# Row sums of a head pair added on TensorE in one episode, and the order written anew around it

## The chip, the cores and the metric

One core of one Trainium2 chip runs the whole kernel in one launch. The metric is the device time of an execution in microseconds (us); a lower number is better. TensorE is called PE here, VectorE DVE, ScalarE ACT, GpSimd POOL and SyncE SP, as in the profile.

## The reference

Two stages follow each other. The first is attention over 8 batches and 8 heads, 1152 keys of 64 features, with queries averaged in pairs (576 per head). The second is a mixture of experts that sends each of the 4608 tokens to one of 8 experts.

```python
q_pool = q.reshape(B, H, S // 2, 2, D).mean(axis=3)
scores = scale * np.matmul(q_pool, k.transpose(0, 1, 3, 2))
scores = scores - np.max(scores, axis=-1, keepdims=True)
attn = np.exp(scores)
attn = attn / (np.sum(attn, axis=-1, keepdims=True) + 1e-09)
x = np.matmul(attn, v)            # then (B, S, H*D) as 4608 tokens of 512
logits = x @ w_gate; expert = argmax(logits); gate = softmax(logits)[expert]
out[token] = gate * (relu(x[token] @ w1[expert]) @ w2[expert])
```

## The kernel before

**Tiles of attention.** A batch has four pairs of heads, and a pair's 576 queries are taken in two halves of 288. For each half there are nine chunks of 128 keys. `scores` (L584 to L642) multiplies a chunk in one *score step*: four matmuls of 64 rows by 64 columns that stand in the four quarters of PE's array (L601). DVE takes the chunk out of PSUM into the tile `s` and keeps its minimum (L606). Then the minimum is spread over the partitions by PE (L624), a bias comes of it on DVE (L630), and ACT raises the half to exponentials in three instructions of three chunks each (L634). `values` (L703 to L721) multiplies the chunks with v, again four matmuls of 64 by 64 for a chunk, a *value step* (L714). Score chunks pass through two PSUM tiles `st`, so a third score step has to wait until DVE has taken the first.

**Row sums.** `chunk_sum` (L664 to L701) adds up the exponentials of a half. POOL folds nine chunks into three in two additions of 1728 numbers a partition (L681, L682, shown as line L680 in the profile, where the helper stands). In the first half of a pair a third addition of 576 numbers brings them down to two. PE then adds over the partitions with columns of ones, in matmuls of 128 rows by 32 columns: four of 288 queries in the first half (L692), four of 288 and four of 144 in the second (L692, L698). The matmuls between one change of shape and the next are called an *episode* here: 64x64 for scores and values, 128x32 for sums and router logits, 64x128 for the transposes of q and k (L546, L552). For the last three pairs of the last batch (`LAST = 3`) POOL is left out, and PE adds all nine chunks itself (`whole`, L670 to L678, shown as L675).

**A batch's sums.** `row_sums` (L723 to L745) copies the sums from PSUM (L729), turns and adds the two query halves of the array with three matmuls against the constant `sums_of` (L735), adds 1e-9 (L741) and takes the reciprocal (L742) into `rec`. `routing` (L760 to L909) then makes logits (L789), turns them (L796), picks experts, ranks the tokens, and has POOL write the tokens into the experts' lists by six indirect DMAs (L893). The token numbers lie in `tok`, which DVE raises by 576 for each batch (L855).

**Into the experts.** While the last batch of attention runs, `first_slots` (L911 to L951) picks the two fullest experts so far; SP loads a list for each, and POOL gathers their tokens (L994). The last batch's list writes wait for those gathers. After attention PE runs the experts' products (L1211, L1242, L1272).

**What sets the order.** Nothing is scheduled by the compiler. `Flow.add` takes steps with an engine, a planned duration, a key and the steps that they wait for, and `Flow.emit` (L120 to L236) plays them through on a clock of its own. Each engine takes the ready step with the lowest key; on PE a step of the shape that stands is preferred to a step of another one, unless its key is higher by more than `KEEP`. The order that comes out is written into the program and does not change at run time. The keys come from the table at L30 to L50.

## Time and profile before

| | |
|---|---|
| median of 3 runs | 1170.93 us (1168.75 to 1171.44) |
| the profiled execution's own time | 1169.15 us |
| its span, first to last instruction | 1167.6 us |
| granted clock of TensorE, mean | 0.996 |
| busy: PE, DVE, ACT, POOL | 98%, 67%, 55%, 69% of the span |

The profile has one execution. Attention takes the stretch up to the last value step, which ends near 717 us; the experts take the rest. In a row of the timeline stand the start, the time until the end of the last instruction, the engine, the line, and what was done how often. PE's matmuls overlap, so the time that a piece takes is the start of the next row less its own start. An fp32 matmul leaves two records, so a step of four matmuls is a row with x8.

### The profile page before, as it was taken

What the parts mean: (1) busy time and instruction counts of PE and PEld (TensorE: products, weight loads), DVE (VectorE), ACT (ScalarE), POOL (GpSimd) and SP (SyncE); (2) the same over time, 40 slices, a digit from 0 to 9 for tenths busy, and PEclk for the clock granted to TensorE, in tenths of its full rate; (3) what the DMA queues carried; (4) which work ended last, traced back from release to release, by engine and by line L of the source; (5) the groups of instructions that cost most, each with busy time, mean ns of one, the idle gap of its engine ahead of it and who ended that gap; (6) DMA issues with size and microseconds to landing.
All of it is one profiled execution on the core that took longest, in us unless ns stands there. A gap on an engine that the chain in (4) does not pass through costs nothing.

```text
span 1167.6 us, 34514 instructions
## 1 busy us (share of the span) xinstructions
PE 1148.6 (98%) x14431; PEld 822.3 (70%) x14431; DVE 778.7 (67%) x2141; ACT 636.4 (55%) x794; POOL 808.7 (69%) x440
## 2 busy tenths in 40 slices
PE   8999999999999999999999999999999999999996
PEld 4565555566566556556556566889998989999985
DVE  6777867868868768768768777975554554636440
ACT  4667667567567667667667457433333342535440
POOL 3989899899899899899899334456656566641010
PEclk9999999999999999999999999999999999999998
DMA  7644334344344344344254334754444344625320
GB/s 183 154 116 115 100 89 122 107 97 124 98 105 123 90 109 121 89 117 127 75 122 130 83 97 124 201 179 122 130 123 128 119 133 119 196 72 181 120 71 20
DMA packets 78052, 138.15 MB, mean 118 GB/s; under 512 B 11321, under 2 KB 35777, under 8 KB 77888
## 3 DMA queue, kind: packets, MB, share of 16 engines
q1 hardware_dynamic: 67904, 115.96, 36.2%
q0 software_dynamic: 9712, 19.64, 5.8%
q8 instruction: 115, 1.88, 0.8%
q14 instruction: 49, 0.40, 0.1%
q10 hardware_dynamic: 272, 0.26, 0.1%
HBM read 115.04 MB, written 21.02 MB: 117 GB/s over the span
## 4 chain that ended last, share of the span: by engine, by line
PE 92%; DVE 4%; issue 2%; ACT 0%; POOL 0%; POOLq 0%; ACTq 0%; DVEq 0%
PE st L601 24%; PE m L714 24%; PE ph L1211 16%; PE py L1272 12%; PE py L1242 5%; PE sums L692 3%; PE st L546 2%; DVE s L606 2%; PE sums L675 1%; PE st L552 1%; DVE w2l L1117 1%; PE st L624 1%; PE sums L789 1%; PE sums L698 1%; PE m L1261 0%
## 5 line engine op out<-in xcount | busy, mean ns | idle before, releaser
L606 DVE TENSOR_SCALAR_CACHE_REDUCE s<-st 128x576 f32<-128x576 f32 x576 | 420.7, 753 | 138.5 <-PE st L601 130.9
L634 ACT ACTIVATE s<-s,bias 128x1728 f32<-128x1728 f32 x192 | 320.1, 1730 | 139.6 <-DVE bias L630 110.1
L601 PE MATMUL st<-qT,kT 64*64 64x288 f32 x4608 | 361.7, 408 | 2.5 <-DVE s L606 1.9
L714 PE MATMUL m<-s,vn 64*64 64x288 f32 x4608 | 356.6, 404 | 0.0
L601 PEld LDWEIGHTS st<-qT,kT 64*64 64x64 f32 x4608 | 163.8, 132 | 134.2 <-DVE s L606 54.5
L714 PEld LDWEIGHTS m<-s,vn 64*64 64x64 f32 x4608 | 172.2, 133 | 86.0 <-issue 1.7
L680 POOL TENSOR_TENSOR fold<-s 128x1728 f32<-128x1728 f32 x58 | 224.3, 3867 | 8.5 <-ACT s L634 8.2
L680 POOL TENSOR_TENSOR fold<-fold,s 128x1728 f32<-128x1728 f32 x58 | 225.0, 3880 | 1.8
L994 POOL DMA_INDIRECT xr<-x_runs,ix x99 | 108.1, 1092 | 87.4 <-DVE s L606 20.9
L1211 PE MATMUL ph<-xh,w1h 128*128 128x384 f32 (+6 forms) x480 | 150.3, 313 | 1.6 <-ACT xh L1162 0.8
L1211 PE MATMUL ph<-xl,w1h 128*128 128x384 f32 (+6 forms) x480 | 148.8, 310 | 0.3 <-DVE xl L1117 0.3
L1211 PE MATMUL ph<-xh,w1l 128*128 128x384 f32 (+6 forms) x480 | 148.4, 309 | 0.0
L1280 POOL DMA_INDIRECT out_dram<-y,rec x41 | 46.2, 1127 | 142.1 <-ACT hh L1218 46.6
L1220 DVE SCALAR_TENSOR_TENSOR hl<-ph,hh 128x384 fp32r<-128x384 f32 (+5 forms) x100 | 55.1, 551 | 98.7 <-ACT hh L1218 98.3
L1218 ACT ACTIVATE hh<-ph 128x384 fp32r<-128x384 f32 (+5 forms) x100 | 48.7, 487 | 122.8 <-PE ph L1211 122.7
L1211 PEld LDWEIGHTS ph<-xh,w1h 128*128 128x128 f32 x480 | 90.6, 189 | 4.3 <-DVE hl L1220 1.7
L1211 PEld LDWEIGHTS ph<-xl,w1h 128*128 128x128 f32 x480 | 90.5, 189 | 1.1 <-DVE xl L1117 0.5
L1211 PEld LDWEIGHTS ph<-xh,w1l 128*128 128x128 f32 x480 | 90.3, 188 | 0.0
L1272 PE MATMUL py<-w2h,hh 128*128 128x512 f32 x224 | 88.7, 396 | 0.0
L1272 PE MATMUL py<-w2h,hl 128*128 128x512 f32 x224 | 88.3, 394 | 0.0
L1272 PE MATMUL py<-w2l,hh 128*128 128x512 f32 x224 | 88.0, 393 | 0.0
L893 POOL DMA_INDIRECT lists<-re,di x48 | 44.7, 931 | 60.1 <-PE m L714 33.1
(190 smaller groups left out, 1442.1 us busy)
## 6 DMA issues: line engine op xcount, KB each, us to landing
raw<-in_moe_w_dram SPq DMA_DIRECT2D x80, 512.0 KB, 4.4
qn<-in_q_dram SPq DMA_DIRECT2D x62, 384.0 KB, 5.6
vn<-in_v_dram SPq DMA_DIRECT2D x32, 576.0 KB, 4.0
kn<-in_k_dram SPq DMA_DIRECT2D x31, 576.0 KB, 5.2
x_runs<-row SPq DMA_DIRECT2D x96, 99.0 KB, 4.3
xr<-x_runs,ix POOLq DMA_INDIRECT x99, 2.7
x_runs<-empty SPq DMA_DIRECT2D x4, 297.0 KB, 7.9
xq<-x_runs,ix POOLq DMA_INDIRECT x49, 2.7
```

Of the source, the lines that this page charges most:

```text
L601: made = nc.tensor.matmul(pt.t[to, h, :HQ], x.kT.t[up, c * P + i * D:c * P + (i + 1) * D], x.qT.t[up, cols], start=True, stop=True, tile_p ...
L606: nc.vector.tensor_scalar(s.t[:, c], pt.t[:, :, :HQ], -SCALE, None, op0=ALU.mult, op1=ALU.min, accum_out=mx.t[:, c:c + 1],)
L634: nc.scalar.activation(s.t[:, c0:c0 + n], s.t[:, c0:c0 + n], AF.Exp, bias=bias.t, scale=-1.0)
L680: add = lambda to, a, b: nc.gpsimd.tensor_tensor(to, a, b, ALU.add)
L714: made = nc.tensor.matmul(pa[i].t[cs, :HQ], x.vn.t[up, h, c, :], s.t[up, c, h], start=c == 0, stop=c == NC - 1, tile_position=(up.start, c ...
L994: return nc.gpsimd.indirect_dma_start(out=x.xr[i // NQD].t[:, i % NQD, :], out_offset=None, in_=xg, in_offset=bass.IndirectOffsetOnAxis(ap ...
L1211: made = nc.tensor.matmul(view()[:, i, :], a[:, c, fp], b[:, c, :n], start=c == 0 and k == 0, stop=c == NDC - 1 and k == 2)
L1218: a = f.add("ACT", act(nb * n) - 44, lambda fs=fs, view=view: nc.scalar.activation(hidden(m)[0][:, fs, :n], view(), AF.Relu), at - 20, don ...
L1220: d = f.add("DVE", dve(nb * n), lambda fs=fs, view=view: nc.vector.scalar_tensor_tensor(hidden(m)[1][:, fs, :n], view(), 0.0, hidden(m)[0] ...
L1242: made = nc.tensor.matmul(py.t[:, :n], a[:, c % 2, ds], b[:, c, :n], start=c == 0 and k == 0, stop=c == NFC - 1 and k == 2)
L1272: made = nc.tensor.matmul(py.t[:n], a[:, c, hs], b[:, c % 2, :], start=c == 0 and k == 0, stop=c == NFC - 1 and k == 2)
L1280: ins = nc.gpsimd.indirect_dma_start(out=out, out_offset=bass.IndirectOffsetOnAxis(ap=x.re.t[:up, r:r + 1], axis=0), in_=y.t[:up], in_offs ...
```

## The change

The two halves of a pair are summed on PE in one piece. POOL folds the first half into `two`, by three additions of 1152 numbers and one of 576, and the second half into `three` as before. PE then runs four matmuls for `two` and eight for `three` behind each other. `LAST` is 2, so one more pair of the last batch is folded on POOL. A batch's sums are turned by three transposes instead of matmuls with `sums_of`; DVE adds the two query halves in one reduction from PSUM, and the small constant (now 0.5e-9 for each half) comes in as the bias of ACT's copy. Token numbers of all batches lie in a table `toks`, so `tok` is no longer raised. The last batch's list writes wait until the early lists are loaded, no longer until the gathers are done. Most keys of the table have new values, and the planned price of a change of shape is 130 in place of 110.

```diff
-FOLD_BUFS = 2
+TWO_BUFS, THREE_BUFS = 2, 1
-K_EXP = 13
-K_SUM = 33
+K_EXP = 37.8
+K_SUM = 25.6
...
-K_FIRST = 51
+K_FIRST = 78.3
...
-LAST = 3
+LAST = 2
...
-SWITCH = 110
+SWITCH = 130
...
-        u = tile_of(o, "fold", [P, 3, 2, HQ], bufs=FOLD_BUFS, pool=o.rt)
         add = lambda to, a, b: nc.gpsimd.tensor_tensor(to, a, b, ALU.add)
+        if half == 0:
+            u = tile_of(o, "two", [P, 2, 2, HQ], bufs=TWO_BUFS, pool=o.rt)
+            p = f.add("POOL", pool(4 * HQ), lambda: add(u.t, s.t[:, 0:2], s.t[:, 2:4]), key, every(ready[:4]), [s, u])
+            for c in (4, 6):
+                p = f.add("POOL", pool(4 * HQ), lambda c=c: add(u.t, u.t, s.t[:, c:c + 2]), key, done(p, *every(ready[c:c + 2])), [s, u])
+            p = f.add("POOL", pool(2 * HQ), lambda: add(u.t[:, 0], u.t[:, 0], s.t[:, 8]), key, done(p, ready[8]), [s, u])
+            sums.two = u, p
+            return None
+        u = tile_of(o, "three", [P, 3, 2, HQ], bufs=THREE_BUFS, pool=o.rt)
         p = f.add("POOL", pool(6 * HQ), lambda: add(u.t, s.t[:, 0:3], s.t[:, 3:6]), key, every(ready[:6]), [s, u])
         p = f.add("POOL", pool(6 * HQ), lambda: add(u.t, u.t, s.t[:, 6:9]), key, done(p, *every(ready[6:])), [s, u])
-        three = half
-        if not three:
-            p = f.add("POOL", pool(2 * HQ), lambda: add(u.t[:, 0], u.t[:, 0], u.t[:, 2]), key, done(p), [u])
+        u2, p2 = sums.two
 
         def total():
...
+            for i, h in grid:
+                put(i, h, 0, u2.t[:, i, h], start=hp == 0, stop=False)
+            for i, h in grid:
+                put(i, h, 1, u.t[:, i, h], start=False, stop=False)
+            for i, h in grid:
+                w = slice(i * HQ // 2, (i + 1) * HQ // 2)
+                put(i, h, 1, u.t[:, 2, h, w], w, start=False, stop=last)
 
-        return f.add("PE", 750 if three else 500, total, key + 15, done(p, *last), [u, sums], COLS)
+        return f.add("PE", 1235, total, key + 15, done(p, p2, *last), [u, u2, sums], COLS)
...
-        p = f.add("ACT", act(HQ) - 44, lambda: nc.scalar.copy(sm.t, sums.t[:, :HQ]), key, summed, [sums, sm])
+        p = f.add("ACT", act(HQ) - 44, lambda: nc.scalar.activation(sm.t, sums.t[:, :HQ], AF.Identity, bias=tiny), key, summed, [sums, sm])
...
-                nc.tensor.matmul(sums.t[:QP, HQ + j * NS:HQ + (j + 1) * NS], sm.t[:, j * QP:(j + 1) * QP],
-                                 sums_of.rearrange("p f a h -> p (f a h)"), start=True, stop=True)
+                nc.tensor.transpose(sums.t[:QP, j * P:(j + 1) * P], sm.t[:, j * QP:(j + 1) * QP], ident)
...
-            nc.vector.tensor_scalar(gs.t, src, 1e-9, None, op0=ALU.add)
-            nc.vector.reciprocal(rec.t.rearrange("p a j h -> p (a j h)"), gs.t.rearrange("p a j h -> p (a j h)"))
+            src = sums.t[:QP, :3 * P].rearrange("p (j u x z) -> p j x u z", j=3, u=2, x=2 * H)[:, :, :, :, 0]
+            nc.vector.tensor_reduce(gs.t, src, axis=AX.X, op=ALU.add)
+            nc.vector.reciprocal(rec.t.rearrange("p f j (a h) -> p j h a f", h=2),
+                                 gs.t.rearrange("p j (h a f) -> p j h a f", h=2, f=2))
...
-        i = f.add("ACT", 200, lambda: nc.scalar.copy(re.t.bitcast(I32)[:, :, 0], tok), at, done(*ready), [re])
+        i = f.add("ACT", 200, lambda: nc.scalar.copy(re.t.bitcast(I32)[:, :, 0], tok if b is None else toks[:, b]), at, done(*ready), [re])
...
-            outs.append(f.carry("POOL", 1230, lambda j=j: enlist(j), at + (K_PUT if b is None or b < B - 2 else 0) * j / NJ, done(p, i, *hold), [di, re], 40, 4400, paced=CALM))
+            outs.append(f.carry("POOL", 1230, lambda j=j: enlist(j), at + (K_PUT if b is None or b < B - 2 else 0) * j / NJ, done(p, i, *listed), [di, re], 40, ENLISTED if b == B - 2 else 4400, paced=CALM))
```

Three places show what became of the order. The first is PE in the second pair of a middle batch, before, where the first half's sums (`fold_5700`) stand between score steps (`st`); value steps are `m`, shown as two rows of x2.

```order
L601 MATMUL st_5899<-qT_5736,kT_5734 64x288 x4
L601 MATMUL st_5905<-qT_5736,kT_5734 64x288 x4
L692 MATMUL sums_5682<-fold_5700,ones_72 32x288 x4
L601 MATMUL st_5917<-qT_5736,kT_5734 64x288 x4
L714 MATMUL m_5855<-s_5568,vn_5013 64x288 x2
L714 MATMUL m_5858<-s_5568,vn_5013 64x288 x2
```

The same pair now: the first half's sums (`two_5689`) stand with the second half's, ahead of the transposes of a later pair's k.

```order
L606 MATMUL st_5962<-qT_5752,kT_5750 64x288 x4
L606 MATMUL st_5967<-qT_5752,kT_5750 64x288 x4
L701 MATMUL sums_5699<-two_5689,ones_72 32x288 x4
L701 MATMUL sums_5699<-three_5853,ones_72 32x288 x4
L701 MATMUL sums_5699<-three_5853,ones_72 32x144 x4
L551 MATMUL st_5991<-ident,kp_5771 128x64 x2
```

The lone piece is gone, and the joint piece has grown by one row.

The second place is PE a few steps behind a middle batch's router logits, as it was.

```order
L714 MATMUL m_5379<-s_5099,vn_4745 64x288 x2
L601 MATMUL st_5530<-qT_5360,kT_5358 64x288 x4
L601 MATMUL st_5543<-qT_5360,kT_5358 64x288 x4
L714 MATMUL m_5548<-s_5213,vn_4745 64x288 x2
L714 MATMUL m_5551<-s_5213,vn_4745 64x288 x2
```

And now:

```order
L725 MATMUL m_5372<-s_5132,vn_4787 64x288 x2
L606 MATMUL st_5540<-qT_5364,kT_5360 64x288 x4
L606 MATMUL st_5550<-qT_5364,kT_5360 64x288 x4
L606 MATMUL st_5565<-qT_5364,kT_5360 64x288 x4
L725 MATMUL m_5570<-s_5237,vn_4787 64x288 x2
L725 MATMUL m_5573<-s_5237,vn_4787 64x288 x2
```

Two score steps in a row have become three.

The third place is POOL in that second pair, before; `qp` is the pooling of a later pair's queries, `lists` a list write.

```order
L680 TENSOR_TENSOR fold_5700<-s_5406 128x1728
L893 DMA lists<-re_5423,di_5644 42240x2
L680 TENSOR_TENSOR fold_5700<-fold_5700,s_5406 128x1728
L680 TENSOR_TENSOR fold_5841<-s_5568 128x1728
L680 TENSOR_TENSOR fold_5700<-fold_5700 128x576
L680 TENSOR_TENSOR fold_5841<-fold_5841,s_5568 128x1728
L498 TENSOR_TENSOR qp_5949<-qn_5455 128x2x6x64
```

And now:

```order
L684 TENSOR_TENSOR two_5689<-s_5456 128x1152
L903 DMA lists<-re_5403,di_5665 42240x2
L684 TENSOR_TENSOR two_5689<-two_5689,s_5456 128x1152
L903 DMA lists<-re_5403,di_5665 42240x2
L684 TENSOR_TENSOR two_5689<-two_5689,s_5456 128x1152
L684 TENSOR_TENSOR three_5853<-s_5608 128x1728
L684 TENSOR_TENSOR two_5689<-two_5689,s_5456 128x576
L684 TENSOR_TENSOR three_5853<-three_5853,s_5608 128x1728
L503 TENSOR_TENSOR qp_5960<-qn_5393 128x2x6x64
```

POOL runs six additions for the pair where it ran five, and a list write has moved in between.

## Rows read from the trace of the kernel before

**Rows 1.** The page, busy time of each engine over the whole span.
```profile
PE 1148.6 (98%) x14431; PEld 822.3 (70%) x14431; DVE 778.7 (67%) x2141; ACT 636.4 (55%) x794; POOL 808.7 (69%) x440
```

**Rows 2.** The page, the chain that ended last, shares by engine.
```profile
PE 92%; DVE 4%; issue 2%; ACT 0%; POOL 0%; POOLq 0%; ACTq 0%; DVEq 0%
```

**Rows 3.** Waits of PE and its weight loads: total us, times, longest us.
```profile
PE st L601 <- DVE s L606: 1.9, 8, 0.4
...
PEld sums L692 <- POOL fold L680: 5.3, 12, 0.5
```

**Rows 4.** Timeline of PE, 336 to 349 us, one pair's two sum pieces.
```profile
339.52 1.20 PE L601 MATMUL st<-qT,kT 64*64 64x288 f32 x16
340.66 0.69 PE L692 MATMUL sums<-fold,ones 128*32 128x288 f32 x8
341.28 0.71 PE L601 MATMUL st<-qT,kT 64*64 64x288 f32 x8
341.82 0.67 PE L714 MATMUL m<-s,vn 64*64 64x288 f32 x8
342.30 0.67 PE L601 MATMUL st<-qT,kT 64*64 64x288 f32 x8
...
345.21 0.67 PE L601 MATMUL st<-qT,kT 64*64 64x288 f32 x8
345.81 0.69 PE L692 MATMUL sums<-fold,ones 128*32 128x288 f32 x8
346.32 0.43 PE L698 MATMUL sums<-fold,ones 128*32 128x144 f32 x8
346.68 0.27 PE L546 MATMUL st<-ident,kp 64*128 64x64 f32 x2
```

**Rows 5.** Timeline of PE, 300 to 326 us: both halves' sums in one piece.
```profile
303.56 1.18 PE L692 MATMUL sums<-fold,ones 128*32 128x288 f32 x16
304.56 0.43 PE L698 MATMUL sums<-fold,ones 128*32 128x144 f32 x8
```

**Rows 6.** Timeline of PE, 690 to 713 us, sums of all nine chunks by PE.
```profile
698.67 2.62 PE L675 MATMUL sums<-s,ones 128*32 128x288 f32 x36
701.22 1.20 PE L601 MATMUL st<-qT,kT 64*64 64x288 f32 x16
```

**Rows 7.** Groups of instructions: count, then busy us, mean ns; then idle before.
```profile
L735 PE MATMUL sums<-sums_of,sm 128*96 128x16 f32 x48 | 5.5, 240 | 0.5 <-ACT sm L729 0.5
L796 PE MATMUL sums<-ident,sm 128*96 128x128 f32 x24 | 4.2, 284 | 0.0
L606 DVE TENSOR_SCALAR_CACHE_REDUCE s<-st 128x576 f32<-128x576 f32 x576 | 420.7, 753 | 138.5 <-PE st L601 130.9 <-PE st L624 2.1
L606 DVE DVE_READ_ACCUMULATOR s<-st 128x1 f32 x576 | 47.6, 83 | 0.0
L634 ACT ACTIVATE s<-s,bias 128x1728 f32<-128x1728 f32 x192 | 320.1, 1730 | 139.6 <-DVE bias L630 110.1 <-POOL fold L680 24.7 <-DVE xr L1154 4.8
```

**Rows 8.** Timeline of PE, 660 to 668 us, a run of five score steps.
```profile
663.07 1.39 PE L601 MATMUL st<-qT,kT 64*64 64x288 f32 x16
664.67 1.40 PE L601 MATMUL st<-qT,kT 64*64 64x288 f32 x16 [0.21 <-DVE s L606]
```

**Rows 9.** Line L680 on POOL: instructions, duration ns min/median/max.
```profile
L680 POOL TENSOR_TENSOR fold<-s x58: 3846/3868/3892, 23.7 to 637.1; 128x1728 f32<-128x1728 f32 x58
L680 POOL TENSOR_TENSOR fold<-fold,s x58: 3845/3882/3912, 27.7 to 641.0; 128x1728 f32<-128x1728 f32 x58
L680 POOL TENSOR_TENSOR fold<-fold x29: 1394/1414/1437, 33.3 to 635.7; 128x576 f32<-128x576 f32 x29
```

**Rows 10.** Busy us of PE, PEld, DVE, ACT, POOL between two batches' logits; clock, DMA.
```profile
288.29:375.02 86.73, 86.70 (x1468) 51.80 (x1464) 66.05 (x199) 57.30 (x65) 79.69 (x31) 1.00 0.42 107
```

**Rows 11.** Timeline of all engines, 296 to 305 us: a spread and its exponentials.
```profile
296.86 0.29 PE L624 MATMUL st<-ident,top 64*64 64x64 f32 x8
...
297.81 4.99 ACT L634 ACTIVATE s<-s,bias 128x1728 f32<-128x1728 f32 x3 [2.53 <-DVE bias L630]
```

**Rows 12.** Timeline of POOL, 600 to 735 us, the first early gather.
```profile
679.00 1.05 POOL L994 DMA_INDIRECT xr<-x_runs,ix  x1 [20.92 <-DVE s L606]
```

More of the change, by code (lines that the diff above doesn't have):

```diff
@@ L56 @@
 LEAD = 55
-AHEAD = 152
+AHEAD = 144.8
 XR2 = 4
@@ L62 @@
 KEEP = 19
-LAST = 3
+LAST = 2
+LISTED = 1500
+ENLISTED = 800
 EXPS = 3
@@ L80, in __init__ @@
         self.kind, self.make, self.left, self.held, self.tile, self.slot = kind, make, 0, False, None, None
+        self.two = None
     @property
@@ L701, in chunk_sum @@
-        return f.add("PE", 750 if three else 500, total, key + 15, done(p, *last), [u, sums], COLS)
+            to = lambda i, h: slice(64 * i + 32 * h, 64 * i + 32 * h + 32)
+            grid = [(i, h) for i in range(2) for h in range(2)]
+            put = lambda i, h, of, src, w=slice(0, HQ), **kw: nc.tensor.matmul(
+                sums.t[to(i, h), w], ones4[:, hp, of, :], src, tile_position=(0, to(i, h).start), **kw)
+            last = hp == NHP - 1
+            for i, h in grid:
+                put(i, h, 0, u2.t[:, i, h], start=hp == 0, stop=False)
@@ L758, with routing @@
     stores, written = [], []
-    def routing(o, f, key, b, xT, rec, sums, ready, hold=()):
+    def routing(o, f, key, b, xT, rec, sums, ready, hold=(), listed=()):
         wk = o.wk
@@ L998, in gather @@
             )
-        p = f.carry(at, 900 if early else 1100, load, key - LEAD, [*known, *stored], [x.re, x.li], 120, 9000 if early else 4000)
+        p = f.carry(at, 900 if early else 1100, load, key - LEAD, [*known, *stored], [x.re, x.li], 120, LISTED if early else 4000)
+        x.listed = p
         p = f.add("DVE", 800, index, key - LEAD, done(p), [x.li, x.ix, x.re])
@@ L1306 @@
         f = Flow(dict(bank=BANKS, st=S_BUFS, s=UNITS, kn=1, qn=1, vn=3, kp=1, qp=1, kT=KT_BUFS, qT=KT_BUFS,
-                      fold=FOLD_BUFS, sums=1, sm=1, xT=2, rec=2, row=ROW_BUFS, lw=1, ex=1, de=1,
+                      two=TWO_BUFS, three=THREE_BUFS, sums=1, sm=1, xT=2, rec=2, row=ROW_BUFS, lw=1, ex=1, de=1,
                       ohb=1, di=2, re=2, rec2=RE_BUFS, li=LI_BUFS, ix=LI_BUFS, xr=XR, xq=XR2, xt=XT, raw=RAW, x=1, **{f"{w}{j}": 1 for w in ("w1", "w2") for j in range(4)}, **{f"h{c}": 1 for c in range(NFC)}, ph=2, py=2, y=Y_BUFS),
-                 ("kT", "qT", "vn", "fold", "s", "st"), ("x", "xt", "xq", *(f"{w}{j}" for w in ("w1", "w2") for j in range(4)), *(f"h{c}" for c in range(NFC)), "ph", "py", "y"), swap_units, in_step)
-        hold = []
+                 ("kT", "qT", "vn", "two", "three", "s", "st"), ("x", "xt", "xq", *(f"{w}{j}" for w in ("w1", "w2") for j in range(4)), *(f"h{c}" for c in range(NFC)), "ph", "py", "y"), swap_units, in_step)
+        hold, listed = [], []
         o.pw = bank(o)
@@ L1331 @@
             outs.append(row_sums(o, f, key, sums, done(*summed), rec, sm, b == B - 1))
-            outs = routing(o, f, key, b, xT, rec, sums, [*outs, router], hold)
+            outs = routing(o, f, key, b, xT, rec, sums, [*outs, router], hold, listed)
             if b == B - 2:
                 hold, first = first_slots(o, f, key + K_FIRST, outs)
+                listed = done(*(x.listed for x in first))
         def swap_pairs():
```

44 lines of the change are left out of this document (16 added, 28 removed).

## The prediction

> **What bounds the kernel now.** I read the busy times first: PE is busy 98% of the span, no other engine more than 69% [rows 1]. The chain that ended last confirms it: 92% of it is PE, and DVE, the next, has 4% [rows 2]. Third come PE's waits: its score steps wait 1.9 us in all for DVE, and the weight loads of the sums 5.3 us for POOL's folds, at most 0.5 us at a time, while matmuls before them still run [rows 3]. So in attention the time is the sum of what PE is given, and an edit is worth what it takes from PE's row or adds to it as a wait. POOL is the engine to keep in view: between two batches' logits it is busy 79.69 us of 86.73 [rows 10].
>
> What PE's pieces take, I read from starts. A step of four matmuls takes 0.48 to 0.49 us (341.82 to 342.30) [rows 4]. A change of shape costs on both sides of it. Ahead of the lone first-half sums two score steps take 1.14 us in place of 0.97, so 0.17 more; the sums take 0.62, so 0.13 more; the step behind them 0.54, so 0.06 more [rows 4]. Ahead of the second half's sums one score step takes 0.60, so 0.11 more [rows 4].
>
> **The change part by part.** The sum below is made against the profiled execution, 1169.15 us; the median of the three runs, 1170.93, stands 1.8 above it, and I carry the difference over to the median.
>
> *Sums in one episode.* Before, a pair pays 0.17 + 0.13 + 0.06 for the lone piece and 0.11 ahead of the joint one. In the order of the change the joint piece stands behind two score steps, which cost 0.17, and it leaves as before. The four extra matmuls take another step: two in a row take 304.56 - 303.56 = 1.00 us [rows 5]. So a pair saves 0.36 + 0.11 - 0.17 = 0.30 us. In the order before I count 23 lone pieces of four sums (the other first halves already stood beside a second half's), and now none. That gives -6.9 us.
>
> *Detours of the transposes.* The order now has three groups of transposes of q and k more that stand alone between steps (a change into them and one out, about 0.3 us each, so 0.9 us) and four that stand between two other small shapes: transposes, sums, transposes. The trace before has no change from transposes into sums. Its bounds are 0 and the 0.13 + 0.06 of the lone piece's leaving; I take 0.17, nearest to the changes on either side of the gap, so 0.7 us. The Trainium skill, in TensorEngine Tiling (Array Packing), Key Properties, says that any change of tiling mode drains the array, while a change of tile alone does not. By that rule these four cost like the rest and the sum stands; if they were free, the sum below would be 5.9 instead of 5.2. The rows of every other change agree with it. Together +1.6 us.
>
> *`LAST` 2.* One pair's two halves leave `whole`. Such a half takes 701.22 - 698.67 = 2.55 us with its leaving [rows 6], 2.41 without, so -4.8 us. The pair now has a joint piece, 1.00 + 0.36 - 0.13 = 1.2 us [rows 4, 5]. Net -3.6 us. POOL gets 17 us of additions more for that pair. What hides them is its idle time of 20.9 us ahead of the first early gather [rows 12]. The six list writes ahead of them now stand between the additions. If that cover is gone, the gathers slip, and the tokens of the first expert are late for PE's first products.
>
> *A batch's sums.* The three matmuls with `sums_of` leave 48 records over 8 batches, 5.5 us busy; three transposes of the same width, which the logits already use, leave 24 and 4.2 us [rows 7]. That is -0.16 us a batch, -1.3 us in all. The reduction and the bias on DVE and ACT replace instructions of the same size and lie beside PE's next steps, so nothing; so does the raise of `tok` that goes, one small DVE instruction a batch.
>
> *POOL's additions.* Three of 1152 numbers and one of 576 replace two of 1728 and one of 576. On the line through 1.41 us for 576 and 3.87 for 1728 [rows 9] one of 1152 takes 2.64, so the pair's first half takes 9.33 in place of 9.16 us: 0.7 us a batch, on top of the 79.7 [rows 10]. PE's batch shrinks to about 86, so POOL stays 5 us short of it. It costs nothing unless a joint piece waits. What that takes: from the spread's start to the exponentials 0.95 us [rows 11], two of them 3.46 [rows 7], then the first addition of `three`, the last of `two` and the second of `three`, 3.87 + 1.41 + 3.88 [rows 9]: 13.6 us. In a steady batch of the new order 27 to 33 score and value steps stand between that spread and the joint sums, and the small pieces among them bring the shortest to about 14.8 us. Before, it was 32 to 35 steps. So 1.2 us are left at the narrowest. In the last batch's two pairs 22 and 26 stand there; the two additions of `three` follow each other directly, 12.2 us, and about 0.3 us is left.
>
> *Runs of score steps.* This is what the new order gives back. There are two `st` tiles, and DVE needs 0.753 + 0.083 us for a chunk [rows 7]. Two score steps take 0.97 us, but in a run the next two start only 664.67 - 663.07 = 1.60 us later [rows 8]: the third step, the fifth and the seventh each pay 0.63. The order before has four runs longer than two (of 4, 5, 6 and 7 steps), which pay 0.63 x 8 = 5.0 us. The new one has twelve: eight of three, two of four, two of seven, which pay 0.63 x 16 = 10.1. Six of those of three stand behind a batch's logits, where before two and two stood apart. So +5.0 us. Bounds: 0 if the values before the run come late anyway, and one more take of 0.84 in each of the eight, 6.7 more.
>
> *The experts.* From a point soon after attention PE's order is the old one, row for row, and the early gathers stand at the same distance from attention's end in it. Nothing.
>
> The sum: -6.9 + 1.6 - 3.6 - 1.3 + 5.0 = -5.2 us. The profiled execution would take 1164.0, the median **1165.7 us**.
>
> **The rivals.**
>
> *A, no new waits.* The third step of a run meets a PE that would have waited for exponentials in any case, or DVE is far enough ahead. For it: waits on PE were next to nothing before [rows 3], in an order from the same planner. Against it: the five-step run did wait [rows 8], and nothing makes a third `st` tile. It gives 1170.93 - 10.2 = 1160.7 us.
>
> *B, nothing is left.* Behind the logits DVE also has the routing's small instructions, so that a run of three waits for one take more, 0.84 us, in eight places. It gives 1165.7 + 6.7 = 1172.4, which is no change. For it: just there the runs were put. Against it: DVE is busy 66 of 86.7 us [rows 10].
>
> *C, slower: joint sums wait for POOL.* PE runs in order, so a joint piece that waits for `three` holds all score and value steps behind it. There are 30 such pieces. The point from which it decides is a mean wait of (5.2 + 2.3) / 30 = 0.25 us. At the longest wait seen on a fold, 0.5 us [rows 3], it costs 15 us and gives 1180.7. For it: 1.2 us of slack, a POOL that is busy 92% of a batch, list writes now among the additions. Against it: the chain of 13.6 us above, and additions whose longest time is within 1.2% of the median [rows 9]. The Trainium skill, SBUF — State Buffer, Terms, says that DVE and GpSimd share a pair of ports that one of them holds for a whole instruction while the other is blocked. A blocked addition would last longer by a DVE instruction; those maxima show none, so the trace does not show this rule at work here.
>
> *D, the change does not do what it says.* The order shows the joint pieces, so I give it nothing.
>
> **How the numbers follow.** A measurement of this kernel can tell about 0.2% from no change, 2.3 us. The forecast (1163 to 1168.5) has 0.47, A 0.24, B 0.18, C 0.11. Faster by over 0.2% (below 1168.6) is the forecast and A, 0.71; the same is B, 0.18; slower is C, 0.11. The range starts at 1159, A with the profiled execution's 1.8 us below the median, and ends at 1172.5, B. It leaves out C and a bit of A.
>
> **What would show it.** Right: joint pieces of about 1.36 us, no lone ones; the time between two batches' logits down from 86.7 to about 86.5 us (0.9 for three joined pieces and 0.16 for the transposes, less 0.17 and 0.63); attention's end some 5 us earlier, the experts' stretch unchanged; in the runs of three a third score step 1.60 us after the first. Wrong: PE waiting for POOL at the joint sums, or the batch no shorter; weight loads of the sums with more than 0.5 us of wait on `three`; PE idle ahead of the first expert products for more than before.

## The result and the profile after

| | before | after |
|---|---|---|
| median | 1170.97 us (4 runs, 1168.75 to 1171.44) | 1184.47 us (4 runs, 1183.05 to 1186.79) |
| ratio | | 1.0119, 95% interval 1.0105 to 1.0133 |
| profiled execution, its span | 1169.15, 1167.6 us | 1184.81, 1183.1 us |

Forecast were 1165.7 us and a range up to 1172.5. The change is slower, by 13.5 us. The two profiled executions differ by 15.7 us, which the rows below divide: 6.6 us up to attention's end and 8.9 behind it.

The page of after, busy time and chain, answers to [rows 1, 2]:

```profile
PE 1147.7 (97%) x14359; PEld 822.3 (69%) x14359; DVE 778.0 (66%) x2134; ACT 636.3 (54%) x794; POOL 838.2 (71%) x476
...
PE 85%; DVE 4%; issue 4%; DMA 3%; ACT 2%; POOL 1%; SPq 0%; POOLq 0%; DVEq 0%; ACTq 0%
```

PE has 0.9 us less to do and the span is 15.5 us longer. So the loss is not more work: PE waits, and the chain says so, with 85% of PE in place of 92%. The waits of PE (total us, times, longest us), beside [rows 3]:

```profile
PE st L606 <- DVE s L611: 8.1, 17, 1.0
PE ph L1222 <- DVE hl L1231: 5.0, 2, 3.0
PE ph L1222 <- ACT xh L1173: 2.2, 2, 1.2
...
PE sums L701 <- POOL three L684: 1.0, 1, 1.0
```

Score steps wait 8.1 us for DVE in place of 1.9. Expert products wait 5.0 us in two places for DVE. The joint sums wait for POOL once, 1.0 us, in the very first pair. Their weight loads show 1.5 us there, one of the prediction's signs of being wrong, and at most 0.5 us in any later pair: rival C is not what happened.

Where in the program? Attention's end (the first expert product) moved from 719.70 to 726.31 us, 6.6 later. From there to the end of the span it takes 456.8 us in place of 447.9, so 8.9 more. The stretches of after, from one batch's logits to the next and from the last but one batch's logits to attention's end, and that last stretch before (columns as in [rows 10]):

```profile
377.31:465.00 87.69, 86.50 (x1466) 51.90 (x1462) 65.29 (x200) 57.29 (x64) 80.34 (x35) 1.00 0.41 107
640.36:726.31 85.95, 81.78 (x1292) 44.67 (x1289) 66.10 (x204) 47.94 (x46) 59.40 (x40) 1.00 0.34 96
```

```profile
635.28:719.70 84.42, 82.55 (x1319) 46.49 (x1316) 60.14 (x196) 47.27 (x56) 38.98 (x33) 1.00 0.35 98
```

A batch takes 87.69 us, where 86.73 stood before [rows 10] and 86.5 was forecast. It grew while the granted clock stayed at 1.00 and PE's busy time shrank by 0.2. The second and the third batch, in which the pattern shown below does not stand yet, take 86.4 us. The stretch ahead of the first batch's logits also grew, from 114.3 to 116.8 us: PE is idle 1.8 us more in it (1.0 at the first joint sums, 0.4 at the first pooled queries), and two more score steps stand ahead of the logits. So the 6.6 us are 2.5 there, -1.1 in the next two batches, 3.7 in the four after them and 1.5 in the last stretch.

**The joint piece is as forecast.** Timeline of PE after, one pair's sums in the last batch, answers to [rows 4, 5]:

```profile
655.58 0.69 PE L701 MATMUL sums<-two,ones 128*32 128x288 f32 x8
656.08 0.91 PE L701 MATMUL sums<-three,ones 128*32 128x288 f32 x16
656.93 0.72 PE L725 MATMUL m<-s,vn 64*64 64x288 f32 x8
```

From 655.58 to 656.93 are 1.35 us (1.36 forecast), and there are no lone pieces.

**The batch: score steps behind the logits.** Timeline of PE and of DVE after, 5 us behind a batch's logits:

```profile
382.12 0.66 PE L725 MATMUL m<-s,vn 64*64 64x288 f32 x8
382.61 0.66 PE L606 MATMUL st<-qT,kT 64*64 64x288 f32 x8
384.26 1.39 PE L606 MATMUL st<-qT,kT 64*64 64x288 f32 x16 [0.99 <-DVE s L611]
385.48 1.64 PE L725 MATMUL m<-s,vn 64*64 64x288 f32 x24
```

```profile
381.51 0.74 DVE L611 TENSOR_SCALAR_CACHE_REDUCE s<-st 128x576 f32<-128x576 f32 x1
382.19 0.08 DVE L611 DVE_READ_ACCUMULATOR s<-st 128x1 f32 x1
382.19 0.87 DVE L825 TENSOR_REDUCE sums<-lw 96x48 f32<-96x384 f32 x1
383.09 0.20 DVE L826 TENSOR_REDUCE lmx<-sums 96x6 f32<-96x48 f32 x1
383.33 0.20 DVE L827 TENSOR_TENSOR ex<-sums,lmx 96x48 f32<-96x48 f32 x1
383.46 0.74 DVE L611 TENSOR_SCALAR_CACHE_REDUCE s<-st 128x576 f32<-128x576 f32 x1
```

The run of three score steps lasts 385.48 - 382.61 = 2.87 us; three steps of 0.485 us are 1.46. So it pays 1.41, where the forecast had 0.63 from a run away from any logits [rows 8]. The difference stands in DVE's rows: from 382.19 to 383.46 DVE works on the batch's routing, and only then takes the chunks whose tiles PE needs. The same place pays 1.40 to 1.41 in five batches. A run of two near 418 us pays 0.41 besides, but not for DVE: it waits for ACT's copy of the turned k, `kT`.

```profile
418.58 0.72 PE L606 MATMUL st<-qT,kT 64*64 64x288 f32 x8 [0.18 <-ACT kT L563]
```

Score steps wait so in seven places of after, 0.41 to 0.42 us each, and in none of before. Without the 1.41 and the 0.41 the batch of 87.69 would take 85.87, which is the forecast of 86.5 without its 0.63.

**The last batch: a pick that takes 2.31 us.** Timeline after, DVE and POOL:

```profile
657.65 2.66 POOL L684 TENSOR_TENSOR two<-s 128x1152 f32<-128x1152 f32 x1 [0.78 <-ACT s L639]
657.84 0.15 DVE L942 TENSOR_REDUCE ffm<-feq 1x1 f32<-1x8 f32 x1
658.02 2.31 DVE L943 TENSOR_TENSOR feq<-feq,ffm 1x8 f32<-1x8 f32 x1
660.26 0.13 DVE L944 TENSOR_SCALAR early<-ffm 1x1 int32<-1x1 f32 x1
```

Eight numbers take 2.31 us, and 0.15 in the pick before. The operation ends as POOL's addition ends. The addition is one of those that `LAST` 2 gives to POOL; before, no pick ran beside an addition, the last of which ended ahead of the first pick. In the change itself PE lost little by it: the takes behind the pick were in time for the score steps at 662.00. A value step beside it came 1.15 us late, which I first put down to the pick; e8 shows that it was ACT. The last batch lost its 1.5 us to that step, to its run behind the logits (1.41) and to others that `LAST` 2 did not make up for; the rows do not divide these further.

**The experts: lists that come late.** Timeline after, POOL and DVE, 24 to 48 us behind the first expert product:

```profile
750.04 1.91 POOL L903 DMA_INDIRECT lists<-re,di  x1 [0.48 <-PE py L1283]
752.83 4.86 POOL L903 DMA_INDIRECT lists<-re,di  x1 [0.88 <-PE py L1283]
753.41 3.48 DVE L1128 TENSOR_TENSOR w1l<-raw,w1h 128x1024 fp32r<-128x1024 f32 x3
757.99 0.91 POOL L903 DMA_INDIRECT lists<-re,di  x1 [0.30 <-issue]
...
767.79 0.78 POOL L988 DMA_DIRECT2D li<-lists  x1 [6.26 <-DVE stab L1116]
...
773.75 0.23 DVE L998 TENSOR_SCALAR ix<-li,gid 128x12 int32<-128x12 int32 x1 [2.97 <-DMA li<-lists]
773.89 0.73 DVE L1001 COPY rec<-li 32x3 int32<-32x3 int32 x4
774.65 0.56 DVE L1231 SCALAR_TENSOR_TENSOR hl<-ph,hh 128x384 fp32r<-128x384 f32 x1
```

The fifth list write takes 4.86 us (median 0.92) and ends 0.80 us behind the end of DVE's row of weight splits. The first write starts 18.4 us behind the first product (before 13.6), the sixth 31.7 (23.5), the first list load 41.5 (29.9). DVE, in order, waits for the loaded list with `ix`, and `hl`, which frees PE, stands behind it. PE is idle for 3.05 us, until 775.26:

```profile
771.70 0.34 PE L1222 MATMUL ph<-xl,w1h 128*128 128x384 f32 x1
771.88 0.34 PE L1222 MATMUL ph<-xh,w1l 128*128 128x384 f32 x1
775.26 0.44 PE L1222 MATMUL ph<-xh,w1h 128*128 128x384 f32 x1 [3.05 <-DVE hl L1231]
...
776.91 0.52 PE L1222 MATMUL ph<-xh,w1l 128*128 128x384 f32 x1
777.23 0.52 PE L1222 MATMUL ph<-xh,w1h 128*128 128x384 f32 x1
```

The stop costs more than its own length. From 776.58 to 779.99 the granted clock of TensorE is 0.50, its lower level of 1.2 GHz, where before has 1.00 in the same products (columns as in [rows 10]):

```profile
776.58:779.99 3.41, 3.41 (x12) 3.41 (x12) 2.19 (x7) 0.49 (x1) 1.02 (x1) 0.50 0.31 87
```

A product then starts every 0.32 us in place of 0.18. An estimate from these rows: 3.41 us hold 10.7 products, each 0.14 us later, so about 1.5 us are lost. It also shows in PE's busy time: behind attention's end PE is busy 437.8 us for as many products as took 435.8 before.

Two more stops follow, when the gathers that hang on these lists are late: 1.2 and 1.9 us. After the last of them the products stay 14.8 us behind those of before, 6.3 of which were there ahead of the first stop.

### The profile page after: what moved, and what is told of

It is laid out like the page before. It is cut to its first block, busy times and chain, and to the rows that moved or that the text cites. A ratio compares the mean times of both kernels' runs of the same rounds, so it can differ in the third digit from the quotient of the medians.

```text
span 1183.1 us, 34387 instructions
## 1 busy us (share of the span) xinstructions
PE 1147.7 (97%) x14359; PEld 822.3 (69%) x14359; DVE 778.0 (66%) x2134; ACT 636.3 (54%) x794; POOL 838.2 (71%) x476
## 4 chain that ended last, share of the span: by engine, by line
PE 85%; DVE 4%; issue 4%; DMA 3%; ACT 2%; POOL 1%; SPq 0%; POOLq 0%; DVEq 0%; ACTq 0%
PE st L606 22%; PE m L725 22%; PE ph L1222 15%; PE py L1283 11%; PE py L1253 5%; PE sums L701 3%; DVE s L611 2%; PE st L551 2%; PE st L557 1%; DMA qn<-in_q_dram 1%; PE sums L680 1%; DMA lists<-re,di 1%; ACT kT L563 1%; PE st L629 1%; PE sums L799 1%
## 5 line engine op out<-in xcount | busy, mean ns | idle before, releaser
L684 POOL TENSOR_TENSOR two<-two,s 128x1152 f32<-128x1152 f32 (+1 forms) x90 | 201.6, 2240 | 2.6
L684 POOL TENSOR_TENSOR three<-s 128x1728 f32<-128x1728 f32 x30 | 115.8, 3860 | 16.2 <-ACT s L639 16.1
L684 POOL TENSOR_TENSOR three<-three,s 128x1728 f32<-128x1728 f32 x30 | 116.3, 3877 | 0.9
L1222 PEld LDWEIGHTS ph<-xh,w1h 128*128 128x128 f32 x480 | 91.0, 190 | 10.2 <-DVE hl L1231 6.1
```

The costliest lines, as they stand in the source:

```text
L684: add = lambda to, a, b: nc.gpsimd.tensor_tensor(to, a, b, ALU.add)
L1222: made = nc.tensor.matmul(view()[:, i, :], a[:, c, fp], b[:, c, :n], start=c == 0 and k == 0, stop=c == NDC - 1 and k == 2)
```

## The experiments

Theory 1: the sums are worth what was forecast, and the new order of the steps took it back: score steps in threes where DVE has the routing, and lists that come late. Theory 2: joint sums, POOL's longer additions or the new row sums cost the time wherever they stand. Theory 3, formed on the way: DVE and POOL hold each other up where both work in SBUF.

On the chips of these runs the kernel before took from 1171 to 1178 us, so each run is compared with before on its own chip, by the ratio; times within a run are as on its chip, in the profiled execution. "List" is the first list load behind the first expert product; "experts" is the time from that product to the end of the span. "Half clock" is the time at a granted clock of 0.50, in the last stretch of attention and in the experts, without the last 10 us of the span, where every run has some.

| run | ratio, interval | attention's end | batch | list | experts | half clock |
|---|---|---|---|---|---|---|
| before | 1 | 719.7 | 86.7 | 29.9 | 447.9 | 0, 0 |
| the change | 1.0119, 1.0105 to 1.0133 | 726.3 | 87.7 | 41.5 | 456.8 | 0, 3.4 |
| e1 | 1.0155, 1.0138 to 1.0172 | 732.6 | 87.8 | 40.6 | 454.1 | 3.4, 6.8 |
| e2 | 1.0123, 1.0106 to 1.0140 | 726.7 | 87.7 | 41.4 | 457.1 | 0, 6.8 |
| e3 | 1.0145, 1.0128 to 1.0162 | 734.7 | 86.4 to 91.0 | 36.6 | 450.6 | 0, 3.4 |
| e4 | 1.0103, 1.0086 to 1.0120 | 725.0 | 87.7 | 35.8 | 452.0 | 0, 3.4 |
| e5 | 1.0046, 1.0030 to 1.0061 | 727.0 | 85.4, 88.7 in turn | 38.7 | 453.5 | 6.8, 3.4 |
| e6 | 1.0030, 1.0018 to 1.0041 | 727.5 | 85.4, 88.6 in turn | 36.3 | 450.7 | 6.8, 0 |
| e7 | 1.0051, 1.0037 to 1.0064 | 732.3 | 86.9 | 28.4 | 448.4 | 3.4, 3.4 |
| e8 | 1.0166, 1.0149 to 1.0183 | 735.2 | 87.7 | 42.7 | 458.9 | 3.4, 10.2 |
| e9 | 1.0056, 1.0036 to 1.0076 | 727.0 | 87.7 | 36.3 | 453.5 | 0, 3.4 |
| e10 | 0.9986, 0.9977 to 0.9995 | 717.7 | 86.0 | 34.7 | 450.8 | 6.8, 3.4 |
| e11 | 0.9987, 0.9978 to 0.9996 | 716.3 | 86.0 | 34.6 | 449.6 | 3.4, 0 |
| e12 | 1.0056, 1.0040 to 1.0071 | 732.8 | 87.9 | 32.9 | 451.8 | 0, 6.8 |

The chips differ in a way that the traces do not explain. The change's order takes 87.7 us for a steady batch in e2 and e4 and also in e8 and e9, although the kernel before takes 1171 us on the chip of the first two and 1177 on that of the others. No trace of before was kept on those chips, so how much of a ratio there belongs to the chip stays open, and the rows of a run count for more than its ratio.

**e1: the new sums, the old table.**

```diff
-K_EXP = 37.8
+K_EXP = 13
...
-K_ROUTE = 55.9
+K_ROUTE = 56
...
-SWITCH = 130
+SWITCH = 110
...
-LISTED = 1500
+LISTED = 9000
```

and so for every number of the table that the change moved, with the list writes waiting for `hold` again.

> The change's code (joint sums of a pair, LAST 2, row sums by transposes, token numbers from a table) with all the order numbers and list rules of before (K_LOAD, K_PIECE, K_MAX, K_EXP, K_SUM, K_ROUTE, K_FIRST, K_SPREAD, AHEAD, SWITCH, LISTED, the list writes' hold). PE's order then has the last batch's logits ahead of the first expert product, but runs of four score steps behind the logits of seven batches. Theory 1 (the loss is made by the new order, not by the joint sums themselves): from the first expert product to the end 447 to 451 us (456.8 in the change, 447.9 before), attention's end 720 to 728 us (726.3 and 719.7), total 1170 to 1178 us. Theory 2 (the joint sums, POOL's longer additions or the new row sums cost the time wherever they stand): both stretches stay as in the change, 1183 to 1186 us.

1188.78 us: a miss for both. The old table under the new sums is no return to the old order. A run of four score steps behind the logits pays 1.49 us a batch (87.8 us), while a run of three 48 us behind the logits pays 0.63 (426.19 in its trace), the price of the forecast: the place sets the price. In the last batch two picks beside POOL's additions take 2.52 and 2.92 us, and PE stands 3.4 us for the takes behind them.

**e2: the old numbers of the experts alone** (`K_FIRST`, `AHEAD`, `LISTED`, `hold`, as in e1).

> The change with K_FIRST, AHEAD, LISTED and the list writes' hold as they were before; the order of attention up to the last two batches stays the change's. PE still has the last batch's logits behind the same first expert products as in the change. Theory 1 (the experts' 8.2 us come from the last batch's routing standing later among the first products, and its list writes and list loads so falling among the weight loads): no help, experts 454 to 458 us, total 1182 to 1186 us. Theory 1b (it is these numbers and rules that put the lists late): experts 447 to 450 us, total 1175 to 1178 us. Attention's end 726 us in both.

1185.55 us, experts 457.1. Theory 1 held: these numbers are not what made the lists late. Timeline of POOL in e2, the sixth list write and the first list load:

```profile
756.61 1.43 POOL L903 DMA_INDIRECT lists<-re,di  x1 [0.30 <-PE py L1283]
...
768.04 0.78 POOL L988 DMA_DIRECT2D li<-lists  x1 [1.97 <-DVE f L1110]
```

No write takes longer than 1.43 us here and the sixth starts at 29.9 us, yet the list load comes at 41.4 us as in the change. So a held write is not needed for late lists: here it is the 11.4 us from the last write to the load.

**e3: the old sums, the new table** (the K_ numbers, `AHEAD` and `SWITCH` of the change in the kernel before).

> The kernel before with the change's order numbers alone (K_LOAD, K_PIECE, K_MAX, K_EXP, K_SUM, K_ROUTE, K_FIRST, K_SPREAD, AHEAD, SWITCH); the sums in lone and joint pieces, LAST 3 and the old row sums stay. Theory 1 (the order makes the loss): slower than before, attention's end 721 to 725 us, the experts 448 to 456 us, total 1173 to 1182 us. Theory 2 (the sums themselves make it): attention and experts as before, 1169 to 1172 us.

1187.70 us, the direction of theory 1 and more than it expected: without a single joint sum of the new kind, the new table costs 16.5 us. Neither kernel bears the other's table (1.0145 here, 1.0155 in e1).

**e4: logits before the second product step.**

```diff
-        p = f.add("PE", 1050, logits, at, ready, [pl, xT], COLS)
+        p = o.logits = f.add("PE", 1050, logits, at, ready, [pl, xT], COLS)
...
-                              done(p, *x.w1_ready[(f0 + i) // 2], *x.turned),
+                              done(p, *([o.logits] if p and f.room is not None else []), *x.w1_ready[(f0 + i) // 2], *x.turned),
```

> The change with one dependency more: of the first expert products only the first step (six products) may stand ahead of the last batch's logits on PE, as before; some 40 rows of PE's order differ, all behind attention, and POOL's order of list writes stays. Theory 1 (late logits make the lists late, and these the gathers): the first list write starts 1 to 4 us earlier behind the first product than in the change (18.4 us there, 13.6 us before), the experts take 449 to 454 us instead of 456.8, total 1177 to 1182 us. Rival (the lists are late for another reason, such as VectorE's longer queue or the weight loads alone): experts 456 to 458 us, total 1184 to 1186 us.

1182.85 us, 1178.60 in the profiled execution. There the list writes run ahead of DVE's splits, none over 1.9 us, the list load comes 5.7 us earlier and the experts take 452.0 us: theory 1, in this execution. The other three took 1182.1 to 1183.7, no trace of them was kept, and over all four the interval overlaps that of the change; the median is 0.85 us above what theory 1 expected. Two of the three have a mean granted clock of 0.992 in place of 0.995; the third has 0.995 as well.

**e5: one number, K_ROUTE 62.**

```diff
-K_ROUTE = 55.9
+K_ROUTE = 62
```

> The change with one number more: K_ROUTE 62 instead of 55.9, so that a batch's routing stands a little later. In PE's order the logits then stand among score and value steps, and the run of three score steps behind them is gone in the steady batches. Theory 1 (a batch of the change is 87.7 us long, not 86.5, because score steps stand three in a row where VectorE also has the routing): batches of 85.5 to 86.5 us on average, attention's end 716 to 720 us (726.3 in the change), experts 452 to 457 us, total 1173 to 1179 us. Theory 2 (the batch is longer by what the joint sums, POOL's longer additions and the new row sums cost): batches stay at 87.7 us, total 1183 to 1186 us.

1182.17 us, on a chip where before takes 1176.19, so 0.46% above it instead of 1.19%. Batches are 87.0 us on average, which is toward theory 1 and short of it: the run behind the logits is gone, but every second batch has another run of three, which pays 0.63, and the waits for `kT` stay. Attention's end is not earlier, because PE stood 4.0 us for DVE's takes in the last batch: ahead of them two picks took 2.10 and 3.12 us, each until one of POOL's additions ended. From the end of that stop on the granted clock is 0.50, for 6.8 us in all. The picks made theory 3.

**e6: both** (the edits of e4 and e5).

> K_ROUTE 62 as in the run beside it, and only one first product step may stand ahead of the last batch's logits. Theory 1: both gains add up, attention's end 716 to 720 us, experts 449 to 454 us, total 1169 to 1175 us. Rival (the experts' time hangs on when the lists come against the weight loads, and that is not set by the logits' place on PE): experts 454 to 458 us, total 1174 to 1179 us.

Ratio 1.0030; its interval overlaps that of e5, and attention's end and the total miss what theory 1 expected. The experts take 2.8 us less than in e5 on the same chip, but e5 has 3.4 us at half clock in them and e6 none. So the gains of e4 and e5 may add up; it is not shown.

**e7: another table** (all K_ numbers, `SWITCH`, `KEEP`, `AHEAD`, `LEAD`).

> The change's code with another table of order numbers (all K_ numbers, SWITCH, KEEP, AHEAD, LEAD differ), under which PE has no run of three score steps behind the logits in the steady batches and the last batch's logits stand ahead of the first expert product. Theory 1 (the sums of a pair in one episode are worth what was forecast, and only the order gave it back): batches of 85.7 to 86.3 us, attention's end 713 to 718 us, experts 446 to 452 us, total 1160 to 1170 us, below the kernel before. Theory 2 (the sums cost time themselves): no table helps by this much, total 1176 us and more.

1182.33 us at before's 1176.19. Half a hit: experts 448.4 us with a list load at 28.4, both the shortest of the changed code; batches of 86.9 us, above the 85.7 to 86.3 expected. The last batch takes 97 us from the logits ahead of it, since no expert product stands ahead of its logits: PE waits 4.7 us there. Two picks took 2.86 and 3.28 us, and PE stood 2.3 us behind the first.

**e8: POOL's additions after the picks.**

```diff
-            p = f.add("POOL", pool(4 * HQ), lambda: add(u.t, s.t[:, 0:2], s.t[:, 2:4]), key, every(ready[:4]), [s, u])
+            p = f.add("POOL", pool(4 * HQ), lambda: add(u.t, s.t[:, 0:2], s.t[:, 2:4]), key, [*every(ready[:4]), *(done(o.picked) if not o.exact and b == B - 1 and hp == 1 else [])], [s, u])
...
-            x.found = p
+            x.found = o.picked = p
```

> The change with one dependency more: POOL's additions for the second pair of the last batch start only after VectorE has picked the two early experts (small VectorE operations of first_slots, on one partition). PE's order differs in 20 rows of the last batch. In the change one of these picks (feq, 0.15 us elsewhere) took 2.31 us, as long as POOL's addition beside it ran, and PE stood 1.15 us for the take behind it. Theory 3 (a VectorE operation with all its operands in SBUF waits for POOL's addition that runs beside it): every pick takes 0.13 to 0.16 us, the 1.15 us stall of PE at 658 us is gone, attention's end 723.5 to 725.5 us (726.3 in the change), total 1182 to 1184 us. Rival (the long pick is chance or a clash with something else): a pick of over 1 us stays, attention's end 726 to 727 us, total 1184 to 1186 us.

1195.73 us. Every pick takes 0.13 to 0.24 us, as theory 3 has it. The rest was a miss: PE's late value step is still there, for ACT's copy behind three exponentials, and the run is the slowest of all. It also has the most half clock. The additions moved and met the next operations of the kind. Timeline of e8, all engines:

```profile
659.02 2.40 PE L725 MATMUL m<-s,vn 64*64 64x288 f32 x34 [0.44 <-ACT xT L730]
...
674.55 3.88 POOL L684 TENSOR_TENSOR three<-s 128x1728 f32<-128x1728 f32 x1
...
676.43 2.04 DVE L998 TENSOR_SCALAR ix<-li,gid 128x12 int32<-128x12 int32 x1
...
679.89 4.41 DVE L998 TENSOR_SCALAR ix<-li,gid 128x12 int32<-128x12 int32 x1
...
680.42 3.84 POOL L684 TENSOR_TENSOR three<-three,s 128x1728 f32<-128x1728 f32 x1
...
685.74 2.88 PE L606 MATMUL st<-qT,kT 64*64 64x288 f32 x20 [4.63 <-DVE s L611]
```

Both `ix`, 0.22 us elsewhere, end where an addition ends (678.43, 684.26); the takes stand behind them, and PE waits 4.63 us. My price for the move was wrong, the mechanism right: it was seen where it had been and where it was sent.

**e9: the second expert's splits after the list writes.** PE's and POOL's orders stay, row for row.

```diff
-                    w.w1, w.w1_ready = split_weights(m, f, w, "w1", at - 40, 8, 0)
+                    w.w1, w.w1_ready = split_weights(m, f, w, "w1", at - 40, 8, 0, [x[9][0] for x in outs[-NJ:]] if i == 1 else ())
```

> The change with one dependency more: the second expert's w1 casts and splits (ACT, VectorE) stand behind the issue of the last batch's six list writes. PE's and POOL's orders are the change's, row for row; 20 rows of VectorE's and 8 of ACT's differ. In the change POOL's fifth list write took 4.86 us, up to the end of a row of three w1l splits on VectorE. Theory 3 (POOL's list write waits for VectorE's splits, both in SBUF, and the lists so come late): no list write over 2 us, the sixth starts 26 to 29 us behind the first expert product (31.7 in the change), the first list load 33 to 38 us behind it (41.5), experts 449 to 453 us instead of 456.8, total 1177 to 1182 us. Rival (the lists are late because the weight loads fill the DMA queues): the list writes are short but the list loads come no sooner than 39 us behind the first product, experts 455 to 458 us, total 1183 to 1186 us.

Ratio 1.0056 in place of 1.0119. Timeline of POOL in e9:

```profile
751.70 1.91 POOL L903 DMA_INDIRECT lists<-re,di  x1 [0.48 <-PE py L1283]
754.49 1.60 POOL L903 DMA_INDIRECT lists<-re,di  x1 [0.88 <-PE py L1283]
756.39 0.91 POOL L903 DMA_INDIRECT lists<-re,di  x1 [0.30 <-issue]
...
763.34 0.79 POOL L988 DMA_DIRECT2D li<-lists  x1
```

The fifth write takes 1.60 us in place of 4.86, the list load comes 36.3 us behind the first product in place of 41.5, the experts take 453.5 us. The sixth write (29.4) and the experts end just outside what was expected. Theory 3 stands on this side too: taking the splits away shortened the write. But the write gives only 2.3 of the 5.2 us; the other 2.9 come between the last write and the load (7.0 us in place of 9.8). The edit moved something else with the splits: four weight loads were issued 26.7 to 30.7 us behind the first product in the change and 32.1 to 35.5 in e9. The rival, weight loads in the way of the lists, expected the load no sooner than 39 us and fell so far; for these 2.9 us it is not excluded.

**e10: a third table, without runs behind the logits** (its numbers stand in the expectation).

> The change's code with a third table of order numbers (K_LOAD -125.2, K_V -103.6, K_POOL 124.4, K_PIECE -20.8, K_TOP -48.9, K_MAX -11.3, K_EXP -12.1, K_SUM 6.9, K_AV 46.6, K_ROW 86, K_ROUTE 65.2, K_CHAIN 150.4, K_FIRST -6.9, K_PUT 157.9, K_SPREAD -29, K_NEXT 124.9, SWITCH 102.5, AHEAD 101.1, LEAD 8.6, K_SLOT 60.7, KEEP 16.5). PE's order has four runs of three score steps and two of six in all (the change: eight of three, two of four, two of seven), none of them behind a batch's logits; the last batch's logits still stand behind the first two product steps. Theory 1 (the joint sums are worth what was forecast, the order took it back): batches of 85.8 to 86.5 us, attention's end 713 to 719 us (719.7 before, 726.3 in the change), experts 449 to 455 us, total 1164 to 1172 us where the kernel before takes 1171 us, or as much higher as it is on the chip of the run. Theory 2 (the sums themselves cost the time): 1178 us and more.

1169.64 us where before takes 1171.21. The changed code is now as fast as before or a little faster (by 0.05% to 0.23%, about the 0.2% that this kernel's measurement can tell), and 1.3% faster than the change with its own table. All ranges of theory 1 held. A batch's stretch and the place behind the logits in e10:

```profile
375.80:461.81 86.01, 86.01 (x1468) 51.99 (x1465) 65.91 (x198) 57.41 (x65) 80.66 (x35) 1.00 0.42 105
```

```profile
382.63 1.15 PE L606 MATMUL st<-qT,kT 64*64 64x288 f32 x16
383.61 1.15 PE L725 MATMUL m<-s,vn 64*64 64x288 f32 x16
384.57 1.15 PE L606 MATMUL st<-qT,kT 64*64 64x288 f32 x16
385.55 1.15 PE L725 MATMUL m<-s,vn 64*64 64x288 f32 x16
```

Two score steps, two value steps, 0.97 us each pair, no wait; PE is busy for the whole batch. POOL is busy 80.66 us of it and the joint sums do not wait: theory 2 falls. In a steady batch the sums give 0.72 us of the 0.89 forecast without the new run. Over the whole kernel only 1.6 us of the forecast's 10.2 without new waits are seen. Two stops of 1.4 and 1.6 us behind a held pick in the last batch, 6.8 us at half clock there and 3.4 more in the experts take much of the rest: the three executions with a mean clock of 0.995 took 1167.9 to 1168.0 us, the eight with 0.992 or 0.993 1168.7 to 1170.9.

**e11: that table with the edits of e4 and e9.**

> The same table, and beside it both dependencies tried alone before: only one first product step ahead of the last batch's logits, and the second expert's w1 splits behind the issue of the last list writes. Theory 1 with theory 3 (late logits and blocked list writes make the experts late): attention's end as in the run beside it, list writes under 2 us each, the first list load 30 to 35 us behind the first product, experts 447 to 451 us, total 1161 to 1169 us where before takes 1171 us. Rival (the experts' time is set by something else): as the run beside it within 1 us.

Ratio 0.9987: no different from e10, as the rival expected. The list load comes at 34.6 us in place of 34.7, so nothing was freed. In the profiled executions the experts take 1.2 us less, but PE makes the same stop of 1.24 us in both, 72 us behind the first product, and only in e10 is it followed by 3.4 us at half clock.

**e12: a control, the old code with another table.**

> A control for the run with the third table: the kernel before, its sums in lone and joint pieces, LAST 3 and its old row sums, with a table of order numbers searched in the same way. PE's order has one run of three score steps, one of six and one of seven, and the last batch's logits stand behind the first product step. Theory 1 (the joint sums are worth what was forecast in an order without new waits): the old sums have nothing to give back, batches stay at 86.5 to 86.8 us, total 0.997 to 1.002 of before, so no better than the changed code with its third table (0.9986 of before). Theory 4 (any searched table gives the gain, the sums are worth nothing): batches of 86.1 us and less, total below 0.996 of before.

Ratio 1.0056, slower than before, with batches of 87.9 us: outside what both theories expected. It speaks against theory 4, that any searched table gives the gain, but weakly: this one table is worse than the old one, and a better one for the old code is not excluded.

## Why the prediction was wrong, step by step

- *Bound by PE in attention*: right, and the reason the loss shows as waits of PE.
- *Sums in one episode, detours, a batch's sums*: right in the steady batch. The piece measured 1.35 us for 1.36, and the batch without its two waits is 85.87 us, as forecast. e10, without the run, has 86.0. The detours' 0.17 us each no run shows alone.
- *POOL's additions*: right in the steady batches, one wait of 1.0 us in the first pair, which the chain of 13.6 us, worked out for a steady batch, did not look at.
- *`LAST` 2*: the cover was only half looked at. "What hides them is its idle time" is about POOL. The additions stand beside DVE's picks, 2.31 us for one of 0.15, and beside `ix`, 1.29 us for 0.22. In the change PE did not wait for these; in the orders of e1, e5, e7, e8 and e10 the same meeting cost 1.4 to 4.6 us. The 3.6 us that `LAST` 2 was to save are not seen: the last stretch is 1.5 us longer.
- *Runs of score steps*: the right mechanism and the wrong size, a step that failed. 0.63 came from a run late in attention, away from any logits [rows 8]. Behind the logits it measured 1.41, so 3.9 us more in five batches. Rival B said just that and put 0.84 us on it where 0.78 was measured. Seven waits for `kT`, 2.9 us, stand nowhere in the sum.
- *The experts, "Nothing"*: the largest step that failed, 8.9 of the 15.5 us. It compared PE's order and the distance of the early gathers. It did not follow the last batch's routing on DVE and the list writes and list loads on POOL, which PE waits for 45 us later. The logits stood one product step later on PE (2.85 us behind the first product in place of 1.80), so that the list writes came later, among DVE's splits, and the longest waited for them. Late lists stopped PE, and about 1.5 of the 8.9 us are the half clock behind the first stop, which no term held. e4 and e9 undid one of the two each; their profiled executions took 4.8 and 3.3 us off the experts.

The forecast for the profiled execution was 1164.0 us and 1184.8 were measured, 20.8 us apart: 8.9 in the experts and 11.8 up to attention's end, which was to come 5.2 us earlier and came 6.6 later. Of the 11.8 the rows name 3.9 in the runs, 2.9 at `kT`, 1.4 in the first batch and 1.15 at ACT's copy; the rest, some 2.4 us, they do not divide.

The rule on the shared ports stood in the prediction, under rival C, and was dismissed by looking at the wrong side. It looked for additions that last longer. In after they still don't (3837 to 3903 ns). The side that is held up here is DVE: each long pick and each long `ix` ends within 0.05 us of the end of an addition. The Trainium skill, SBUF — State Buffer, SBUF: two separate sides, says that the one which starts first holds the pair for its whole instruction and the other stands still. The traces agree in part. In the change the pick starts 0.37 us behind the addition that holds it, and `ix` 2.6 us behind. But the `ix` of 4.41 us in e8 starts at 679.89, 0.53 us ahead of the addition of 680.42, while a gather of POOL still runs; in e1, e5, e6, e7, e10 and e11 one pick each starts 0.27 to 0.62 us ahead of its addition, during a list write. So the recorded starts, which are rough on POOL, do not show that it is always the second one which is held. For the list write of 4.86 us beside splits only its own rows speak.

What stays open: what differs between the executions of e4, what makes some chips slower, and how much of the wait from the last list write to the list load (9.8 us in the change, 7.0 in e9, 6.4 before) is the weight loads that move at the same time. Neither was tried alone.

## What to carry to other kernels

An edit of an order written by a planner is costed on every in-order queue between the moved step and its last reader, not on the bound engine alone: the largest loss here came over POOL's list writes and DVE's index operation. A wait read from a quiet place can be too small for a busy one (0.63 us and 1.41 here). A stop can cost more than its length, so the granted clock behind it is read too. And a table of keys is fitted to its steps: judge a new way of computing with a table set for it, here worth 1.3%, before it is judged at all.

## What was not expected of the hardware

DVE operations on eight numbers took 2.0 to 3.3 us, and an index addition of 128x12 took 4.41, each until POOL's addition ended, while DVE's takes, which read PSUM, kept their time beside the additions of the change (0.71 to 0.76 us). The other way round, an indirect DMA issued by POOL took 4.86 us beside three weight splits on DVE. In a steady batch of the change none of DVE's operations shows it; it came when small SBUF work met a long addition. In e3, the old code, it does stand in steady batches: the raise of `tok` took 0.94 us for 0.16 until POOL's pooling of queries ended. And the granted clock fell to 0.50 for 3.4 to 6.8 us at or just behind many stops of PE, but not at all of them: after the same stop of 1.24 us it fell in e10 and not in e11.
